# Turning the attention output, the spatial weights and part of q by DMA transposes instead of TensorE transposes, with more products on GpSimd and a split tail

## The chip, the cores and the metric

One core of one Trainium2 chip. The metric is device time in microseconds (us) of one execution. A kernel is always compared with the kernel before it, run in the same rounds on the same chip. Single executions fall into a fast and a slow state (the kernel before: about 170.5 us, or about 173 us with a lower granted TensorE clock); only the times of fast ones are compared. The granted clock is the share of full speed at which the chip lets TensorE run, 1.00 being full speed.

## The reference, cut to what matters

```python
# attention: 4 batches, 8 heads, 768 rows, head width 64, blocks of 96 rows
P = sort_net                                   # 8x8 per head, five row/column normalisations
for _ in range(5): P = exp(P - max); P /= rows; P /= columns
k_sorted = einsum('bhij,bhjcd->bhicd', P, k_blocks)     # v likewise
attn = softmax(scale * q_b @ k_sorted^T)                # inside a block of 96
x = (attn @ v_sorted)                                   # -> (4, 768, 512)
# gated MLP
h = relu(x @ w_in);  u, v = halves of h                 # 512 each
v_n = (v - mean) / sqrt(var + 1e-6)
v_s = einsum('ts,bsd->btd', w_spatial, v_n) + b_spatial # 768x768 spatial weights
out = (u * v_s) @ w_out
```

TensorE contracts over partitions. So `x` has to be turned before it meets `w_in`, `w_spatial` before it meets `v_n`, and q and k before the scores. Who does the turning is what the change is about.

## The kernel before: the parts that the change and the argument touch

The schedule is a string of units, given to the engines in this order. A unit is `name : PSUM bank : engine that evicts (A ScalarE, D VectorE, P GpSimd) : arguments`. `L` loads, `QT` turns a pair of q heads, `KT` and `VM` mix k and v with the sort matrix, `VC` rearranges v by small DMAs, `SC` and `AT` are scores and attention output, `XT` turns x, `WS` the spatial weights, `VP` and `UP` are the two halves of the first projection, `LA` normalises v, `SP` is the spatial product with bias and gate, `OP` the output. Other names in the cuts do not matter to the argument.

```python
# order, cut: batch 0's end and batch 1's start
AT:1:0:2:1 XT:7:A:0:0:1 PD:1:4:8 PD:1:0:4 AT:5:0:3:1 ... WS:3:D:3 WS:4:A:0
WS:1:D:1 WS:7:A:2 AT:5:0:1:1 L:k:1:0:128 XT:0:A:0:1:1 WS:3:D:4 VP:2:D:0:2 WS:4:A:5 ...
# order, the tail
SP:1:D:3:1 SP:4:D:3:3 SP:1:D:3:0 SP:4:D:3:2 OP:4:A:3:0 OP:1:D:3:1 OP:4:A:3:2

def u_WS(ps, eng, n):                     # 6 TensorE transposes, one eviction
    for c in range(G):
        nc.tensor.transpose(t[:, 0, c*128:(c+1)*128], wsp_nat[:, c, n*128:(n+1)*128], ident)
    copy(eng, wspT[:, n], t[:, 0, 0:S])

def u_QT(ps, eng, b, hp, ih):             # 12 matmuls against the identity, one eviction
    ...
def u_XT(ps, eng, b, ih, kp):             # 8 TensorE transposes of 96x128, one eviction
    ...
def u_L(what, *a):                        # loads: all issued by GpSimd, in its order
    nc.gpsimd.dma_start(...)
def u_VC(b, ih):                          # v rearranged: 4 small DMAs, issued by SyncE
    for i in range(ih*NI, ih*NI+NI):
        nc.sync.dma_start(out=..., in_=vm[b % 2][i*TB:(i+1)*TB]...)
def u_AT(ps, b, hp, ih):                  # product with 1/sum always on VectorE
    ...
def u_LA(b, n):                           # normalisation always on VectorE
    ...
```

The softmax here doesn't subtract the row's maximum and nothing guards it: scores larger than these inputs give would overflow.

## Time and profile before

| | before |
|---|---|
| time, median of 4 runs | 170.54 us (170.31 to 170.74) |
| span in the profile, mean TensorE clock | 170.2 us, 0.972 |
| TensorE busy | 149.7 us, 88% |
| GpSimd busy | 34.0 us, 20% |

The profile is of one execution, which took 171.97 us; its span, from the first to the last instruction, is 170.2 us. The page's main rows are shown in the prediction below. Two more lines of the page of before matter later: the packet sizes, and the queue that SyncE's DMAs go through (packets, MB, share of 16 engines' span).

```profile
DMA packets 21027, 21.59 MB, mean 127 GB/s; under 512 B 912, under 2 KB 17808, under 8 KB 21008
q1 hardware_dynamic: 6144, 9.13, 16.8%
```

And three windows of 5 us of before (start and end, length; busy us and number of instructions of TensorE, weight loads, VectorE, ScalarE, GpSimd; granted clock; DMA share; GB/s moved). TensorE is busy throughout at full clock, while the loads run at 205 GB/s or more.

```profile
35.00:40.00 5.00, 4.95 (x56) 3.26 (x55) 3.78 (x8) 3.92 (x6) 0.00 (x0) 1.00 1.30 205
40.00:45.00 5.00, 4.95 (x46) 2.75 (x46) 4.34 (x9) 4.02 (x7) 0.88 (x1) 1.00 1.29 205
45.00:50.00 5.00, 5.00 (x90) 3.43 (x89) 4.02 (x8) 4.66 (x9) 0.00 (x0) 1.00 1.24 255
```

### The profile page before, as it was taken

Reading aid. Unit: us, or ns where it says so; the run is one execution under the profiler, and the core shown is the slowest. Engines: PE = TensorE matmul, PEld = TensorE weight load, DVE = VectorE, ACT = ScalarE, POOL = GpSimd, SP = SyncE. Lnnn points to the kernel's source line nnn. Section 1 sums busy time; section 2 is a strip of 40 time slices with the busy share of each in tenths; the row PEclk is TensorE's granted clock in tenths of the full one; section 3 lists DMA queues with packets and bytes.
Section 4 is the critical chain, followed back from the end, with each engine's and each line's share of the span. In section 5 each row is a group of like instructions: output and inputs, shape, how many; then the busy total and the mean of one; then the engine's idle time right before and its main releaser. Section 6 shows DMA issues by size and latency. Waiting matters only on the chain.

```text
span 170.2 us, 4241 instructions
## 1 busy us (share of the span) xinstructions
PE 149.7 (88%) x1785; PEld 95.4 (56%) x1797; DVE 122.8 (72%) x253; ACT 89.6 (53%) x133; POOL 34.0 (20%) x41
## 2 busy tenths in 40 slices
PE   0485697999999999999999999999999999999660
PEld 0344586984756668745557566655557644455320
DVE  3784775787879789778896898569788649739420
ACT  3414676676998519656569134476653247520120
POOL 7929913202000035050000030300003300000000
PEclk9999997599999999999999999999999999999996
DMA  2999999999999992929333000823240000360063
GB/s 28 164 191 204 207 214 203 205 203 207 212 275 231 214 234 23 178 24 161 123 129 123 4 0 9 149 36 123 96 155 0 4 0 0 123 247 4 0 231 143
DMA packets 21027, 21.59 MB, mean 127 GB/s; under 512 B 912, under 2 KB 17808, under 8 KB 21008
## 3 DMA queue, kind: packets, MB, share of 16 engines
q0 software_dynamic: 14864, 12.19, 46.5%
q1 hardware_dynamic: 6144, 9.13, 16.8%
q8 instruction: 14, 0.23, 0.5%
q14 instruction: 5, 0.04, 0.1%
HBM read 24.78 MB, written 6.29 MB: 183 GB/s over the span
## 4 chain that ended last, share of the span: by engine, by line
PE 76%; DMA 8%; DVE 7%; issue 3%; ACT 2%; POOL 2%; ACTq 0%; POOLq 0%; DVEq 0%
PE ps L483 15%; PE ps L471 12%; PE ps L430 12%; PE ps L504 10%; DMA v_in<-in_v_dram 7%; PE ps L389 5%; PE ps L366 5%; PE ps L293 4%; PE ps L411 4%; PE ps L278 3%; DVE gt L495 2%; DVE z L489 2%; DMA out_dram<-o_sb 2%; PE ps L338 2%; PE ps L326 2%
## 5 line engine op out<-in xcount | busy, mean ns | idle before, releaser
L374 ACT ACTIVATE ex<-ps 96x768 bf16<-96x768 f32 x32 | 24.6, 804 | 17.7 <-PE ps L366 17.0
L483 PE MATMUL ps<-wspT,v_sb 128*128 128x384 bf16 x192 | 33.4, 326 | 0.0
L495 POOL TENSOR_TENSOR gt<-z,u_sb 128x768 bf16<-128x768 f32 x7 | 11.5, 1643 | 80.7 <-DVE rec L396 44.5
L483 PEld LDWEIGHTS <-v_sb 128*128 128x128 bf16 x192 | 18.1, 98 | 11.5
L504 PE MATMUL ps<-w_out_sb,gt 128*128 128x512 bf16 x91 | 21.8, 379 | 2.0 <-DVE z L489 1.1
L471 PE MATMUL ps<-xT,w_in_sb 128*128 128x384 bf16 x128 | 23.0, 326 | 0.0
L397 DVE TENSOR_TENSOR x_sb<-ps,rec 96x512 bf16<-96x512 f32 x32 | 22.0, 686 | 1.1
L430 PE MATMUL ps<-w_in_sb,xT 128*128 128x512 bf16 x89 | 21.8, 379 | 0.5 <-issue 0.2
L108 ACT COPY o_sb<-ps 128x1024 f32<-128x1024 f32 x11 | 11.1, 1011 | 19.5 <-PE ps L504 16.6
L489 DVE TENSOR_TENSOR z<-ps,b_bc 128x768 f32<-128x768 f32 x16 | 15.3, 956 | 7.4 <-PE ps L483 7.4
L444 DVE BATCH_NORM_STATS2 stats<-v_sb 128x6 f32<-128x512 bf16 x24 | 16.3, 679 | 3.2 <-ACT v_sb L114 2.9
L471 PEld LDWEIGHTS <-w_in_sb 128*128 128x128 bf16 x128 | 11.9, 98 | 7.9
L278 PE MATMUL ps<-ident,q_in 128*64 128x128 bf16 (+1 forms) x240 | 8.4, 217 | 8.3 <-DMA q_in<-in_q_dram 6.4
L504 PEld LDWEIGHTS <-gt 128*128 128x128 bf16 x96 | 8.8, 97 | 11.7 <-DVE gt L495 1.4
L114 ACT ACTIVATE u_sb<-ps 128x768 bf16<-128x768 f32 x12 | 9.7, 811 | 10.1 <-PE ps L471 9.9
L430 PEld LDWEIGHTS <-xT 128*128 128x128 bf16 x96 | 8.9, 98 | 9.3
L389 PE MATMUL ps<-vb,ex 96*128 96x65 bf16 x256 | 12.8, 199 | 0.1
L389 PEld LDWEIGHTS <-ex 96*128 96x128 bf16 x256 | 11.1, 101 | 2.6 <-issue 0.3
L278 PEld LDWEIGHTS <-q_in 128*64 128x64 bf16 (+1 forms) x240 | 6.9, 115 | 9.8 <-DMA q_in<-in_q_dram 6.4
L116 DVE TENSOR_SCALAR v_sb<-ps 128x1024 bf16<-128x1024 f32 (+1 forms) x7 | 8.0, 1147 | 5.5 <-PE ps L430 5.3
L366 PEld LDWEIGHTS <-kT 64*96 64x96 bf16 x256 | 8.0, 124 | 5.3 <-issue 3.9
L366 PE MATMUL ps<-qT,kT 64*96 64x96 bf16 x256 | 10.7, 215 | 0.2 <-ACT ex L374 0.2
(73 smaller groups left out, 197.5 us busy)
## 6 DMA issues: line engine op xcount, KB each, us to landing
out_dram<-o_sb SPq DMA_DIRECT2D x12, 512.0 KB, 2.8
k_in<-in_k_dram POOLq DMA_DIRECT2D x4, 768.0 KB, 14.3
v_in<-in_v_dram POOLq DMA_DIRECT2D x4, 768.0 KB, 21.9
vb<-vm SPq DMA_DIRECT2D x24, 99.0 KB, 5.5
q_in<-in_q_dram POOLq DMA_DIRECT2D x3, 768.0 KB, 20.4
wsp_nat<-in_moe_w_spatial_dram POOLq DMA_DIRECT2D x1, 1152.0 KB, 21.6
w_in_sb<-in_moe_w_in_dram POOLq DMA_DIRECT2D x2, 512.0 KB, 14.7
q_in<-in_q_dram POOLq DMA_DIRECT2D x2, 384.0 KB, 8.7
```

Source lines behind the costliest of these rows:

```text
L278: nc.tensor.matmul(t[hh * 64:hh * 64 + 64, g * n:(g + 1) * n], lhsT=st["q", b][lo:lo + n, 2 * hp + hh, g * D:(g + 1) * D], rhs=ident[lo:lo ...
L366: nc.tensor.matmul(t[0:BLK, hh, ii * BLK:(ii + 1) * BLK], lhsT=kT[rows, i * BLK:(i + 1) * BLK], rhs=qT[rows, i * BLK:(i + 1) * BLK], start ...
L374: nc.scalar.activation(out=e[:, 0:2 * NI * BLK].rearrange("p (h c) -> p h c", h=2), in_=t[0:BLK, :, 0:NI * BLK], func=AF.Exp, scale=scale,)
L389: nc.tensor.matmul(t[:, hh, ii * VW:ii * VW + D + 1], lhsT=e[:, c:c + 128], rhs=vb[b % 2][:, ih * NI + ii, 2 * hp + hh, 0:D + 1], start=Tr ...
L397: nc.vector.tensor_mul(out=x_sb[:, :, hp * 128:hp * 128 + 128].rearrange("p i (h d) -> p h i d", h=2), in0=tv[:, :, :, 0:D], in1=_raw_ap(r ...
L430: nc.tensor.matmul(t[:, x, :], lhsT=st["xT", b][:, kc, n * 128:(n + 1) * 128], rhs=w_in_sb[:, kc, DH:DFF], start=(kc == 0), stop=(kc == KC ...
L444: nc.vector.bn_stats(out=stats, in_=v_sb[:, x, :])
L471: nc.tensor.matmul(t[:, x, 0:HW], lhsT=w_in_sb[:, kc, mc * 128:(mc + 1) * 128], rhs=st["xT", b][:, kc, ih * HW:(ih + 1) * HW], start=(kc = ...
L483: nc.tensor.matmul(t[:, x, 0:HW], lhsT=st["v_sb", b, n][:, mc * 128:(mc + 1) * 128], rhs=wspT[:, n, x * HW:(x + 1) * HW], start=(n == 0), ...
L489: nc.vector.tensor_add(out=z.rearrange("p (x c) -> p x c", x=2), in0=t[:, :, 0:HW], in1=b_bc.rearrange("p (x c) -> p x c", x=2),)
L495: eng.tensor_mul(out=gt, in0=z, in1=st["u", b, mc // 2][:, mc % 2])
L504: nc.tensor.matmul(t[:, x, :], lhsT=st["gt", b, mc][:, c * 128:(c + 1) * 128], rhs=w_out_sb[:, mc, :], start=(mc == 0), stop=(mc == FC - 1),)
```

## The change

The intent: TensorE bounds the middle of the kernel, and part of its work is turning data. DMA engines, mostly idle after 62 us, can turn data while they move it. So all spatial weights, x of batches 1 to 3 and q of batches 2 and 3 are turned by DMA, issued by SyncE; ten attention products and most normalisations go to GpSimd, which was 20% busy; batch 0's q is loaded by halves of the heads; and the last spatial unit and the last outputs are halved to one PSUM bank each (`SH` and `OH` in the cut). The whole order was laid out anew. The core of the diff:

```diff
+    def u_WX(c):                       # six of these in place of six WS
+        nc.sync.dma_start_transpose(out=wspT[:, :, c*128:(c+1)*128], in_=wsp_nat[:, c, :])
+    def u_XX(b, ih):                   # six in place of twelve XT (batches 1 to 3)
+        nc.sync.dma_start_transpose(out=x_tile(b, ih)..., in_=st["x", b, ih]...)
+    def u_QX(eng, b):                  # two in place of eight QT (batches 2 and 3)
+        for hh in range(2): ...        # two copies put q in the order the DMA wants
+        nc.sync.dma_start_transpose(out=st["qX", b]..., in_=qx...)
 def u_AT(ps, eng, b, hp, ih):
+        if eng == "P":                 # ten of 32
+            nc.scalar.copy(out=xr, in_=tv[:, :, :, 0:D + 1])
+        (nc.gpsimd if eng == "P" else nc.vector).tensor_mul(...)
 def u_LA(eng, b, n):
+        if eng == "P":                 # fifteen of 24
+            nc.gpsimd.tensor_scalar(out=nm, in0=mv[:, n, 0:1], scalar1=-1.0, ...)
+            nc.gpsimd.tensor_scalar(out=v_sb, in0=v_sb, scalar1=nm, scalar2=rs, ...)
 # order, cut
-WS:1:D:1 WS:7:A:2 AT:5:0:1:1 L:k:1:0:128 ...
+PD:1:4:8 SC:6:0:2:1 ... PD:2:4:8 AT:2:D:0:1:1
+L:v:1:0:128 AT:6:P:0:2:1 SC:0:0:0:1 VT:4:D:3:0 L:k:1:0:128 ...
+SC:2:0:3:0 SC:0:0:1:0 PD:3:4:8 WX:5 ... AT:0:P:0:1:0 ... L:q:1:0:128 ... WX:3 ... WX:0
 # tail
-SP:1:D:3:1 SP:4:D:3:3 SP:1:D:3:0 SP:4:D:3:2 OP:4:A:3:0 OP:1:D:3:1 OP:4:A:3:2
+SP:0:D:3:1 SP:2:D:3:2 SP:0:P:3:0
+SH:2:D:3:3:0 SH:3:D:3:3:1 OH:0:A:3:1 OH:3:D:3:0 OH:2:A:3:4 OH:0:A:3:2 OH:3:A:3:3 OH:2:A:3:5
```

## The prediction

> **What bounds the kernel now.** I read the page first (busy time, then the 40 slices, then the chain that ended last), then the groups kept apart by shape, then the chain in order of time, and last the tail.
>
> ```profile
> PE 149.7 (88%) x1785; PEld 95.4 (56%) x1797; DVE 122.8 (72%) x253; ACT 89.6 (53%) x133; POOL 34.0 (20%) x41
> PE   0485697999999999999999999999999999999660
> PEclk9999997599999999999999999999999999999996
> DMA  2999999999999992929333000823240000360063
> ...
> PE 76%; DMA 8%; DVE 7%; issue 3%; ACT 2%; POOL 2%; ACTq 0%; POOLq 0%; DVEq 0%
> ```
>
> TensorE is at 9 tenths in nearly every slice from about 30 us to 157 us, and 76% of the chain is TensorE. So in the middle a TensorE instruction that goes is time that goes, if nothing makes TensorE wait in its place. The DMA engines are full to about 62 us (the loads of three batches and all weights) and mostly idle later. The head to 15.6 us is loads: the chain stands 11.5 us on v. The granted clock dips at 25 to 34 us.
>
> Busy time misleads for small matmuls: a transpose of x shows 215 ns, but they overlap. What a unit costs is read from the chain in order of time (columns: start us, us, what):
>
> ```profile
> 31.51 0.64 PE ps L411 x8
> 33.23 1.91 PE ps L257 x24
> ...
> 71.26 0.79 PE ps L411 x16
> ...
> 92.03 0.34 PE ps L278 x12
> ...
> 135.86 0.68 PE ps L411 x16
> ```
>
> A unit of 8 transposes of x costs 0.34 to 0.40 us at full clock (0.64 in the slow stretch), a q unit of 12 costs 0.34, and the 36 of the spatial weights cost 1.91 + 0.34 + 0.34 = 2.59 us.
>
> The tail is bound by VectorE, not TensorE:
>
> ```profile
> 151.56 0.97 DVE z L489
> 152.55 0.94 DVE gt L495
> ...
> 157.35 0.96 DVE z L489
> 158.33 0.97 DVE gt L495
> 159.30 0.05 issue
> 159.35 1.48 PE ps L504 x6
> 160.86 0.04 issue
> 160.90 1.02 ACT o_sb L108
> 161.94 2.76 DMA out_dram<-o_sb
> 164.79 1.01 ACT o_sb L108
> ```
>
> Four pairs of bias-add and gate go through VectorE one after the other while TensorE waits; then three two-bank outputs, two of them evicted by ACT in 1.01 us each. The last eviction also waits for an output buffer still being written out.
>
> **What the Trainium skill says.** (1) "Advanced Engine Details and Errata", X-Bar Transpose (TRN2): transposing DMAs run as fast as plain ones, 350 to 400 GB/s; "DMA: Bandwidth & Descriptors", Latency and other measured facts, has 261 GB/s for a non-contiguous case, and its Anatomy section a fixed cost near 2 us per DMA. Nothing in the trace before transposes by DMA; its plain 512 KB stores landed in 2.8 us and its small v rearrangements in 5.5 us (median), which fits a fixed cost plus queueing. (2) "GPSIMD Engine Reference", 4.1: two-input elementwise work is about twice as slow there, and GpSimd has no way into PSUM, which is why the moved attention products need a ScalarE copy first. The trace agrees: the gate took 1643 ns on GpSimd and 958 ns on VectorE. (3) "SBUF — State Buffer", on the shared port pair: a VectorE op in a two-port mode or with two SBUF inputs and a GpSimd op lock each other out. The GpSimd row before, 20% busy, does not show how much that costs.
>
> **The change part by part.**
>
> TensorE. x: 128 transposes become 32 (batch 0 keeps its four units). The chain pieces of the twelve units of batches 1 to 3 are 0.68 + 0.79 + 0.34 + 0.34 + 0.79 + 0.34 + 0.34 + 0.68 = 4.3 us. Spatial weights: 36 go, 2.6 us. q of batches 2 and 3: eight units of 0.34, 2.7 us. q of batch 0: eight half units become four full ones, of which the two that v's arrival does not hide save some 0.4 us. Added on TensorE: nothing; the scores of batches 2 and 3 read q in runs of 16 columns and all scores write to 128-column places, which I take as free. Sum: **10.0 us off the TensorE path**.
>
> VectorE. Off: 10 attention products of 0.686 (6.9), 15 normalisations of 0.404 (6.1), 4 x copies of 0.55 (2.2), 3 weight copies (1.7), 4 full and 4 half q copies (3.8 + 2.2), one v_sb relu (1.2): 24.1. On: three more full gates and two halves (3.9), 3 v copies, one each of u, vm, two outputs and the mix copy (5.4), and four copies of 128x1536 that put q in the order the DMA wants (estimate 1 us each, three times the 404 ns of a 128x512 one-input op and rounded down: 4). Net about -11, so 112 us of 159: 70%, as before, not a bound.
>
> ScalarE. Off: 8 x copies (6.4), 3 weight copies (2.4), 4 half q (1.9), others 7.7; on: ten copies of 96x520 from PSUM (0.58 each, from the 577 ns of its 96x512 copy: 5.9), five single-bank outputs (3.0), one relu (1.0). Net -8.5, to 81 us.
>
> GpSimd. Off: 4 gates of 1.64 (6.6). On: 10 products at 1.1 (two thirds of 1643 ns), 15 normalisations at 0.7 (its one-input 512-column copy took 622 ns) plus small negations: some 24. Net +17, to 51 us. Beside TensorE, unless a product it does is the last piece of an x block.
>
> DMA. Added: 6 weight transposes of 197 KB, 6 of x of 393 KB, 2 of q of 786 KB, 5.1 MB on SyncE's queue. Estimated landing, with 2 us plus bytes at 261 GB/s: 2.8, 3.5 and 5.0 us. The order leaves room: between the last attention product of an x block and its first reader stand some 7.6 us of TensorE work (for the last block three spatial units of 1.95 and a v pair of 1.73), less about 1 us for the product itself and its queue. q has over 10 us. The weight transposes fall in the saturated stretch but the first spatial unit now comes later, after all of batch 1's attention.
>
> Tail. From the end of the first of the last spatial units, before: 170.2 - 151.5 = 18.7 us. After, with the same durations: three full units and two halves end TensorE's part at 5.9; GpSimd's gate of unit 0 starts at 4.9 and ends at 6.5, VectorE's last half gate at about 6.9 but only the second half of the rows needs it; six single-bank outputs of 0.865 from 6.6 end at 11.8; a one-bank copy 0.6; a 256 KB store some 2.4; and the 1.6 us that also follow the last landing before: 16.4. **2.3 us** off.
>
> Sum: 170.4 - 10.0 - 2.3 = 158.1. I put back about 1 us: waits that the removed work had covered (in the batch-0 stretch at 19 to 30 us TensorE is already only 70 to 80% busy, so some of what goes there goes into idle time). **159 us**.
>
> **Rivals.** (a) A transpose takes the place of the transposes: the wait for a landing replaces the 0.34 us units. For: eight transposes lie on the path by data, SyncE issues in order, so one x block stands behind four v rearrangements that wait for their own inputs, and the small v copies took 5.5 us rather than 2. Against: 7.6 us of cover. If a landing takes 10 us, four late ones cost 2.5 us each: 169. (b) The saturated DMA stretch binds: 1.2 MB of weight transposes push back the loads of batch 1. By bytes at the observed rate those loads come some 5 us ahead of their use now; the transposes would take 3 to 6 us of that, and TensorE gets there sooner. If half of it shows: 162 to 163. Against: several of those readers stand later in the new order. (c) GpSimd becomes the bound in places: a product there takes a copy (0.58), a reciprocal (0.2) and 1.1 us instead of 0.9, behind normalisations and 0.9 us DMA issues, and under the port lock. For: the normalisations feed the spatial units directly. Against: 32% busy. It would cost 1 to 3 us: 160 to 162. (d) Better than the sum: the VectorE stop at 50.9 to 53.6 us (u, then k, then vm on the chain, 2.7 us) and two stops inside units that show no releaser (1.9 and 1.0 us) go as well: 155.
>
> **Range and chances.** The sum of what goes rests on chain pieces, so it is good to 1 us; (b) and (c) each have perhaps one chance in four, (a) in its full form one in twelve, (d) in part one in three. That gives 159, and 155.3 to 163 for eight in ten. Faster by over 2% (below 167) needs only a third of the sum: 0.95; within 2%: 0.04; slower: 0.01.
>
> **What would show it.** Right: TensorE's busy time falls to about 140, its slices stay at 9 from about 35 us to the tail, the chain has no line for transposed x, q or weights above 1 us, landings of x stay below 6 us, the tail from the first of the last spatial units to the end is near 16.4 us. Wrong: TensorE idle before the v or u projections with a DMA into xT as releaser (a), or before batch-1 mixes with k or v loads (b), or before spatial units with GpSimd's v_sb or the products' x_sb (c); score matmuls of batches 2 and 3 slower than 0.25 us a unit.

## The result, and the profile after

| | before | after |
|---|---|---|
| time, median of 4 runs | 170.54 us | 179.78 us (178.58 to 181.51) |
| span of the profiled execution, mean TensorE clock | 170.2 us, 0.972 | 179.7 us, 0.922 (slow state) |
| ratio of fast runs, 95% interval | | 1.0519 (1.0455 to 1.0583) |

A ratio here is the mean time of one kernel's fast runs over the mean of the other's fast runs of the same rounds, so it is not quite the ratio of the medians. The result is correct in both. The change made the kernel 5% slower; the prediction was 159 us and gave "slower" one chance in a hundred.

The profiled execution of after is its slowest, in the slow state: 181.51 us, where the three fast ones took 178.58 to 180.24. The big waits read from it below are not of that state: e4, further down, has the same order up to 65 us, was profiled in the fast state and waits 9.96 us on q, 1.84 on v and 2.47 on k. From the page of after:

```profile
PE 145.6 (81%) x1506; PEld 88.0 (49%) x1519; DVE 114.1 (63%) x230; ACT 81.9 (46%) x124; POOL 52.9 (29%) x77
PE   0395999981089459954999999999999999999890
PEclk9997999999669655897899999999999999999999
DMA  2999999999999999999995419795316610035044
...
DMA packets 41490, 26.67 MB, mean 148 GB/s; under 512 B 21377, under 2 KB 38273, under 8 KB 41473
...
q1 hardware_dynamic: 26608, 14.24, 39.2%
...
PE 46%; DMA 32%; issue 11%; POOL 4%; DVE 2%; POOLq 1%; ACT 1%; SPq 0%; ACTq 0%; DVEq 0%
```

Three things stand out (a slice is 4.5 us here). TensorE has holes between 40 and 85 us (slices 1 and 0, then 4 and 5, then 5 and 4), where the row before had 9 throughout; its clock falls after each hole. The DMA row stays at 9 to about 94 us instead of 64. And SyncE's queue now takes 39.2% of the DMA engines' time instead of 16.8%, for only 5.1 MB more, in 20,464 more packets; packets under 512 B grew by as many. DMA's share of the chain went from 8% to 32%.

Where TensorE stood still, from its timeline in after (start us, length us, line, operation, output<-inputs, count, and in brackets the idle time before it and what ended it). L320 is q, L384 and L335 mix v and k, L485 and L530 are the two projections, L542 is the spatial product:

```profile
39.82 1.48 PE L530 MATMUL ps<-xT,w_in_sb 128*128 128x384 bf16 x8
49.92 2.13 PE L320 MATMUL ps<-ident,q_in 128*64 128x128 bf16 x36 [8.62 <-DMA q_in<-in_q_dram]
...
60.90 0.82 PE L384 MATMUL ps<-v_in,pd 128*128 128x384 bf16 x2 [2.30 <-DMA v_in<-in_v_dram]
...
67.05 0.85 PE L335 MATMUL ps<-pd,k_in 128*64 128x128 bf16 x12 [1.98 <-DMA k_in<-in_k_dram]
...
70.73 3.38 PE L542 MATMUL ps<-wspT,v_sb 128*128 128x384 bf16 x12
...
83.25 0.39 PE L485 MATMUL ps<-w_in_sb,xT 128*128 128x512 bf16 x1 [4.42 <-DMA xT<-x_sb]
```

With one more of 0.77 us on k at 39.03 these are 18.1 us of waits on DMA. The timeline of before has none over half a microsecond after 30 us on a DMA; its own q unit follows without a wait:

```profile
45.35 1.62 PE L278 MATMUL ps<-ident,q_in 128*64 128x128 bf16 x48
```

The same windows as above, in after. TensorE is nearly empty from 41 to 50 us, and all that while the DMA engines are busy but move half as much as before:

```profile
35.00:40.00 5.00, 4.17 (x43) 2.29 (x43) 3.27 (x5) 2.79 (x6) 3.83 (x6) 1.00 1.38 116
40.00:45.00 5.00, 1.30 (x8) 0.59 (x6) 1.19 (x4) 1.91 (x3) 2.92 (x4) 1.00 1.57 101
45.00:50.00 5.00, 0.08 (x2) 0.08 (x4) 0.00 (x0) 0.00 (x0) 0.00 (x0) 0.60 1.36 144
```

What the transposes took is in the DMA issues of after (number, median us from issue to landing) and in SyncE's timeline, whose length here is the time that SyncE itself is held by issuing:

```profile
wspT<-wsp_nat SPq DMA_TRANSPOSE x6, 12.2
xT<-x_sb SPq DMA_TRANSPOSE x6, 4.0
qX<-qx SPq DMA_TRANSPOSE x2, 11.5
```

```profile
29.00 10.86 SPq L301 DMA_TRANSPOSE wspT<-wsp_nat  x4
...
69.45 1.28 SPq L188 DMA_TRANSPOSE xT<-x_sb  x1
72.40 15.40 SPq L181 DMA_TRANSPOSE qX<-qx  x1
...
106.42 3.55 SPq L181 DMA_TRANSPOSE qX<-qx  x1
```

A weight transpose landed after 9.6 to 15.9 us, where 2.8 had been estimated. Of the six of x, all but the first took 3.8 to 4.7 (3.5 estimated); the first, still among the loads, took 13.8. Of the two of q, one took 17.5 among the loads, and the other 5.5 at 106 us, when the loads were over (5.0 estimated). The estimates were those of idle DMA engines.

Last, GpSimd's timeline shows when loads were issued. In before, batch 1's q:

```profile
20.39 0.94 POOL L155 DMA_DIRECT2D q_in<-in_q_dram  x1
```

In after, the same load, with a moved product in front of it:

```profile
32.30 1.04 POOL L454 TENSOR_TENSOR x_sb<-xr,rec 96x512 bf16<-96x512 f32 x1 [2.51 <-DVE rec L453]
33.29 0.94 POOL L154 DMA_DIRECT2D q_in<-in_q_dram  x1
```

GpSimd runs in order: where a product waits for its reciprocal (2.51 us here, 5.06 at 24.70 us), the load behind it waits too. q of batch 1 is issued 12.9 us later than before, and its reader comes about 4 us earlier (the q unit could have started at 41.3 us instead of 45.35).

**The theories after the result.** (T1) The transposes of the weights, put among the loads, slow the loads and hold SyncE, which also issues the v rearrangements; (T2) the products on GpSimd delay the load issues; (T3) a transpose is late for its own reader (x at 83.25 us). The rival to T1: any 1.2 MB added among the loads would cost the same, or late weights as such do the damage.

### The profile page after: what moved, and what is told of

It is laid out like the page before. It is cut to its first block, busy times and chain, and to the rows that moved or that the text cites. A ratio compares the mean times of both kernels' runs of the same rounds, so it can differ in the third digit from the quotient of the medians.

```text
span 179.7 us, 3709 instructions
## 1 busy us (share of the span) xinstructions
PE 145.6 (81%) x1506; PEld 88.0 (49%) x1519; DVE 114.1 (63%) x230; ACT 81.9 (46%) x124; POOL 52.9 (29%) x77
## 3 DMA queue, kind: packets, MB, share of 16 engines
q1 hardware_dynamic: 26608, 14.24, 39.2%
## 4 chain that ended last, share of the span: by engine, by line
PE 46%; DMA 32%; issue 11%; POOL 4%; DVE 2%; POOLq 1%; ACT 1%; SPq 0%; ACTq 0%; DVEq 0%
DMA k_in<-in_k_dram 17%; PE ps L485 9%; PE ps L542 9%; DMA xT<-x_sb 8%; PE ps L530 7%; DMA v_in<-in_v_dram 6%; PE ps L591 6%; PE ps L335 4%; PE ps L442 4%; PE ps L417 3%; PE ps L372 2%; DMA out_dram<-oh_sb 1%; PE ps L577 1%; POOLq L634 1%; PE ps L384 1%
## 5 line engine op out<-in xcount | busy, mean ns | idle before, releaser
L542 PE MATMUL ps<-wspT,v_sb 128*128 128x384 bf16 x180 | 32.2, 335 | 0.0
L485 PE MATMUL ps<-w_in_sb,xT 128*128 128x512 bf16 x87 | 23.0, 400 | 5.3 <-DMA xT<-x_sb 4.4
L454 POOL TENSOR_TENSOR x_sb<-xr,rec 96x512 bf16<-96x512 f32 x10 | 10.5, 1045 | 49.4 <-DVE rec L453 48.5
L530 PE MATMUL ps<-xT,w_in_sb 128*128 128x384 bf16 x128 | 23.5, 326 | 0.0
L542 PEld LDWEIGHTS <-v_sb 128*128 128x128 bf16 x180 | 17.5, 100 | 11.9 <-issue 1.3
L516 POOL TENSOR_SCALAR v_sb<-v_sb,nm,rstd 128x512 bf16<-128x512 bf16 x15 | 11.9, 792 | 28.4 <-ACT rstd L507 18.6
L548 DVE TENSOR_TENSOR z<-ps,b_bc 128x768 f32<-128x768 f32 x15 | 14.3, 953 | 8.5 <-PE ps L542 8.3
L320 PE MATMUL ps<-ident,q_in 128*64 128x128 bf16 x96 | 5.0, 267 | 15.0 <-DMA q_in<-in_q_dram 15.0
L591 PE MATMUL ps<-w_out_sb,gt 128*128 128x512 bf16 x69 | 16.6, 379 | 0.2
L485 PEld LDWEIGHTS <-xT 128*128 128x128 bf16 x96 | 9.1, 102 | 15.3 <-DMA xT<-x_sb 4.8
L454 DVE TENSOR_TENSOR x_sb<-ps,rec 96x512 bf16<-96x512 f32 x22 | 15.1, 687 | 0.8
L530 PEld LDWEIGHTS <-w_in_sb 128*128 128x128 bf16 x128 | 11.8, 98 | 7.8
L107 ACT CAST vm<-ps 128x768 bf16<-128x768 f32 x9 | 7.0, 803 | 13.1 <-PE ps L384 13.1
L113 ACT ACTIVATE v_sb<-ps 128x1024 bf16<-128x1024 f32 (+1 forms) x7 | 6.7, 962 | 11.5 <-PE ps L485 11.4
L554 DVE TENSOR_TENSOR gt<-z,u_sb 128x768 bf16<-128x768 f32 x12 | 11.6, 968 | 0.4
L320 PEld LDWEIGHTS <-q_in 128*64 128x64 bf16 x96 | 4.0, 140 | 16.0 <-DMA q_in<-in_q_dram 15.3
L107 ACT CAST qT<-ps 128x768 bf16<-128x768 f32 x7 | 5.4, 799 | 13.6 <-PE ps L320 13.6
## 6 DMA issues: line engine op xcount, KB each, us to landing
w_in_sb<-in_moe_w_in_dram POOLq DMA_DIRECT2D x2, 512.0 KB, 15.9
```

The costliest lines, as they stand in the source:

```text
L107: nc.scalar.copy(out=out, in_=in_)
L454: (nc.gpsimd if eng == "P" else nc.vector).tensor_mul(out=x_sb[:, hp].rearrange("p i (h d) -> p h i d", h=2), in0=tv[:, :, :, 0:D], in1=_r ...
L485: nc.tensor.matmul(t[:, x, :], lhsT=x_tile(b, n // 3)[:, kc, n % 3 * 128:(n % 3 + 1) * 128], rhs=w_in_sb[:, kc, DH:DFF], start=(kc == 0), ...
L516: nc.gpsimd.tensor_scalar(out=v_sb, in0=v_sb, scalar1=nm[:, 0:1], scalar2=rs[:, n:n + 1], op0=ALU.add, op1=ALU.mult)
L530: nc.tensor.matmul(t[:, x, 0:HW], lhsT=w_in_sb[:, kc, mc * 128:(mc + 1) * 128], rhs=x_tile(b, ih)[:, kc], start=(kc == 0), stop=(kc == KC ...
L542: nc.tensor.matmul(t[:, x, 0:HW], lhsT=st["v_sb", b, n][:, mc * 128:(mc + 1) * 128], rhs=wspT[:, n, x * HW:(x + 1) * HW], start=(n == 0), ...
```

## The experiments

Fourteen kernels gave a result, all correct. Diffs named "order" change only the string of units. All times:

| run | what it is | median us | ratio to before, 95% interval |
|---|---|---|---|
| e1_ws_on_pe | after, weights on TensorE | 174.11 | 1.0205 (1.0161 to 1.0249) |
| e2_before_plus_wx | before, weights by DMA | 186.64 | 1.0931 (1.085 to 1.1012) |
| e3_no_gpsimd_products | after, products on VectorE | 180.40 | 1.0588 (1.0529 to 1.0646) |
| e4_x_q_on_pe | after, x and q on TensorE | 193.87 | 1.1372 (1.1328 to 1.1416) |
| e5_ws_x1_on_pe | e1, batch 1's x on TensorE | 174.00 | 1.0102 (1.0017 to 1.0186) |
| e7_dummy_turn_late | before, dummy transposes at 90 us | 171.35 | 1.0032 (1.0 to 1.0063) |
| e8_dummy_copy_in_loads | before, dummy copies among loads | 175.84 | 1.0268 (1.0198 to 1.0339) |
| e9_dummy_turn_in_loads | before, dummy transposes there | 186.99 | 1.0949 (1.0926 to 1.0972) |
| e10_dummy_turn_after_vb | as e9, behind batch 1's v | 176.63 | 1.0289 (1.0215 to 1.0362) |
| f0_tail_only | before, split tail | 171.42 | 0.9864 (0.978 to 0.9949) |
| f1_late_turns_tail | f0, late x and q by DMA | 169.29 | 0.988 (0.9763 to 0.9997) |
| e11_no_gpsimd_no_early_turns | e5, products on VectorE | 175.65 | 1.0304 (1.0231 to 1.0378) |
| e12_loads_ahead | e5, loads issued ahead | 169.82 | 0.9939 (0.9913 to 0.9966) |
| e13_placed | e12, turns placed anew | 165.26 | 0.9705 (0.9678 to 0.9732) |

Before ran at medians of 170.45 to 170.95 us beside them. The medians include slow runs (two of four in f0 and in f1); the ratios do not.

### Which transposes cost: the weights back on TensorE

```diff
 # order, from after
-WX:5 ... WX:3 ... WX:0 ... WX:2 ... WX:4 ... WX:1
+     ... WS:7:D:0 ... WS:0:A:1 ... WS:2:D:2 WS:3:A:3 ... WS:0:D:4 ... WS:4:A:5
```

> The changed kernel with the six DMA transposes of the spatial weights given back to TensorE (6 units of 6 transposes, 2.6 us), all else as changed. Theory L (transposes of the weights take DMA time from the loads while these fill the DMA engines, and q, v and k of batches 1 and 2 come late): the 8.6 us wait for q at 41 to 50 us goes, the landing of the loads is back near that of the kernel before, and the time falls from 179.8 to 160 to 167 us. Theory X (the x and q transposes and the in-order SyncE queue are what costs): stays above 174. Theory G (GpSimd's products stand in front of the load issues and delay them): stays above 174.

Measured: 174.11 us, by the ratios 5.4 us less than after (1.0519 less 1.0205, of 170.5), though TensorE got 36 transposes back. It missed 160 to 167 us. The wait of 8.62 us on q is gone; the one on x is not. TensorE's and SyncE's timelines of e1:

```profile
42.55 1.20 PE L320 MATMUL ps<-ident,q_in 128*64 128x128 bf16 x36
...
74.59 3.60 PE L485 MATMUL ps<-w_in_sb,xT 128*128 128x512 bf16 x8 [6.11 <-DMA xT<-x_sb]
```

```profile
61.42 3.60 SPq L188 DMA_TRANSPOSE xT<-x_sb  x1
65.13 9.98 SPq L181 DMA_TRANSPOSE qX<-qx  x1
```

The first x transpose was issued at 61.42 us, 7 us before TensorE had come to its reader (68.48), and landed 13.1 us later; the DMA engines moved 191 GB/s from 65 to 70 us. So T1 and T3 both hold, for the same reason: the time at which a transpose runs. The loads show T1 directly. They were issued at the same times in both kernels, to 0.2 us (batch 1's q at 33.48 us in e1 and 33.29 in after, batch 2's v at 35.16 and 34.97), and landed 8 to 11 us earlier in e1: batch 1's q at 41.9 us and not 49.9, v of batch 2 at 52.6 and not 60.9, its k at 56.4 and not 67.0.

### The weights by DMA alone, in the kernel before

```diff
 # order, from before
-WS:3:D:3 WS:4:A:0 WS:1:D:1 WS:7:A:2 ... WS:3:D:4 ... WS:4:A:5
+WX:0 WX:1 WX:2 WX:3 ... WX:4 ... WX:5
```

> The kernel before with one part of the change alone: spatial weights turned by six DMA transposes in the place of the TensorE units. Theory L: TensorE work falls by 2.6 us, but the loads of batches 1 and 2 land about 8 to 12 us later and TensorE waits for them: 174 to 182 us. Theory X or G: loads unharmed, 167 to 169 us.

Measured: 186.64 us, 9% slower than before, with nothing else changed, and worse than the 174 to 182 expected. SyncE's timeline of e2:

```profile
28.96 22.28 SPq L264 DMA_TRANSPOSE wspT<-wsp_nat  x6
51.36 2.97 SPq L358 DMA_DIRECT2D vb<-vm  x4
```

SyncE was held for 22.28 us by six issues. Batch 1's v rearrangements, which in before go out at 41.94 us, go out at 51.36, and TensorE waits 4.54 us on them at 61.94 and in several smaller pieces after, besides 2.28 us on q and 3.19 on v. One part of the change by itself costs more than the whole change.

### Products back on VectorE

```diff
 # order, from after: every AT:_:P and LA:P
-AT:6:P:0:2:1 ... LA:P:0:4 ...
+AT:6:D:0:2:1 ... LA:D:0:4 ...
```

> The changed kernel with all attention products and normalisations back on VectorE (gates stay). Theory G: the loads are issued earlier, TensorE's waits for q, v, k go, 165 us or less. Theory L: the DMA engines are full either way, so earlier issue brings the loads no nearer: 176 to 182 us.

Measured: 180.40 us, as slow as after. But the waits moved. q of batch 1 is issued at 22.73 us instead of 33.29, and TensorE waits 1.04 us on it, not 8.62. In its place, from TensorE's timeline of e3:

```profile
52.17 0.20 PE L442 MATMUL ps<-vb,ex 96*128 96x65 bf16 x1 [3.13 <-DMA vb<-vm]
...
68.10 4.00 PE L542 MATMUL ps<-wspT,v_sb 128*128 128x384 bf16 x12 [3.81 <-DMA wspT<-wsp_nat]
```

So T2 is true of the q wait, which took both causes together: e1 removes it by taking the transposes away, e3 by issuing the load earlier. As the cause of the whole time, T2 alone falls. The last line also shows turned weights that came too late for their own reader, by 3.81 us.

### x and q back on TensorE, weights still by DMA

```diff
 # order, from after
-XX:1:1 QX:D:2 XX:1:0 QX:D:3 XX:2:1 XX:2:0 XX:3:0 XX:3:1
+XT:2:A:1:1:0 XT:6:D:1:1:1 ...  (two XT for each XX, four QT for each QX, at the same places)
```

> The changed kernel with x and q of batches 1 to 3 turned on TensorE again (12 units of 8 and 8 of 12 transposes, 7.0 us more TensorE work), the weights still by DMA. Theory L: the waits for q at 41 us and for v and k at 58 to 67 us stay, the 4.4 us wait for turned x goes, time 178 to 186. Theory X: waits after 65 us go, 168 to 174 us.

Measured: 193.87 us, outside the 178 to 186 that I had expected and on the bad side. The waits on q (9.96), v (1.84) and k (2.47 us) stay, so they are not from the x and q transposes; the wait on x's DMA goes. But the units that I put in its place stand right behind the products that feed them (TensorE waited 2.40 and 0.71 us there in batch 1), and they are 7 us of work (4.3 + 2.7). TensorE's busy time rose from 145.6 to 154.9 us, 9.3 of the 12.8 us between the spans of the two profiles (192.5 and 179.7); the rest is TensorE standing still, and was not split further. The run clears the late transposes of the early waits and no more.

### Weights and batch 1's x on TensorE

```diff
 # order, from e1
-XX:1:1 ... XX:1:0
+XT:2:A:1:1:0 XT:6:D:1:1:1 ... XT:2:A:1:0:0 XT:6:D:1:0:1
```

> The changed kernel with the weights and batch 1's x (four units) given back to TensorE; q of batches 2 and 3 and x of batches 2 and 3 stay on DMA. Theory L, now wider (any transpose by DMA issued before the loads are done, near 75 us, lands late and pushes the loads): the 6.1 us wait for turned x at 68 us and the low clock after it go, 163 to 168 us. Rival (what is left is GpSimd and the tail): stays at 172 to 175.

Measured: a ratio of 1.0102, still not faster than before, and outside the 163 to 168 us expected. Its interval overlaps that of e1, so the step from e1 is not clear of noise. No transpose is now among the loads before 65 us, and yet the loads dip. Windows of e5 (profiled in the slow state; the fast profile of e1 has 161 and 188 GB/s there):

```profile
35.00:40.00 5.00, 4.77 (x41) 3.00 (x43) 2.37 (x5) 2.33 (x5) 2.46 (x4) 1.00 1.20 163
40.00:45.00 5.00, 4.39 (x82) 3.35 (x83) 3.93 (x7) 4.57 (x7) 4.22 (x7) 1.00 1.18 187
```

163 and 187 GB/s, not 205, with GpSimd busy at products. That is T2 seen alone; e12 below tests it.

### Is it the transposing, the bytes, or the place? Three dummies in the kernel before

These keep the weights on TensorE and add six DMAs of the same 197 KB from `wsp_nat` into a tile that nobody reads. No reader can wait for them: what they cost is contention.

```diff
+    scr = const.tile([128, G, S], BF16, name="scr")
+    def u_DX(c):   # transpose
+        nc.sync.dma_start_transpose(out=scr[:, :, c*128:(c+1)*128], in_=wsp_nat[:, c, :])
+    def u_DC(c):   # plain copy of the same bytes
+        nc.sync.dma_start(out=scr[:, c, :], in_=wsp_nat[:, c, :])
 # e7: six DX together ahead of KT:0:A:3:2:2, at 90 us, the loads over
 # e8: one DC ahead of each WS;   e9: one DX ahead of each WS
```

> The kernel before plus six DMA transposes of the weights into a tile that nobody reads, issued near 90 us, when the DMA engines are mostly idle. Theory L: each lands in under 4 us and the time stays within 1% of before. If transposes by DMA are costly wherever they stand: over 2% slower.

> The kernel before plus six plain copies of the same 197 KB pieces, in rows of 1536 bytes, into a tile that nobody reads, issued when the weights have landed, in the load stretch. If only bytes count: 1.2 MB at the 205 KB a us of that stretch push the loads by 5.8 us, of which the slack of some 5 us covers most: 170 to 173 us. If these cost as much as the transposes: over 178.

> The same with six DMA transposes in place of the copies, in the load stretch, TensorE still turning its own weights. If transposing among the loads is what costs: 180 to 190 us, as with the weights turned only by DMA (186.6). If in that run the late weights themselves were what TensorE waited for: below 174.

SyncE's timeline and the DMA issues of e7 (transposes, idle DMA engines):

```profile
89.60 9.12 SPq L266 DMA_TRANSPOSE scr<-wsp_nat  x6
...
scr<-wsp_nat SPq DMA_TRANSPOSE x6, 3.7
```

of e8 (plain copies among the loads):

```profile
28.66 4.37 SPq L270 DMA_DIRECT2D scr<-wsp_nat  x6
...
scr<-wsp_nat SPq DMA_DIRECT2D x6, 192.0 KB, 7.2
```

of e9 (transposes among the loads), with TensorE's longest wait:

```profile
28.86 22.43 SPq L266 DMA_TRANSPOSE scr<-wsp_nat  x6
...
scr<-wsp_nat SPq DMA_TRANSPOSE x6, 14.3
...
62.01 0.24 PE L400 MATMUL ps<-vb,ex 96*128 96x65 bf16 x1 [6.08 <-DMA vb<-vm]
```

| six times 197 KB | SyncE held | median landing | GB/s at 35 to 45 us | cost by the ratio |
|---|---|---|---|---|
| transposes, late (e7) | 9.12 us | 3.7 us | | 0.5 us, at the edge of nothing |
| copies among loads (e8) | 4.37 us | 7.2 us | 265, 213 | 4.6 us |
| transposes among loads (e9) | 22.43 us | 14.3 us | 191, 157 | 16.2 us |

(The cost is the ratio less one, times before's 170.7 us.) The copies add to the traffic, 265 GB/s against before's 205; the transposes take away from it. So the rival "any bytes would do it" accounts for 4.6 of 16.2 us. (At 175.84 us, e8 is outside the 170 to 173 expected of bytes alone.) And e9 is as slow as e2 although its weights come from TensorE: late weights as such are not what made e2 slow.

Where is the rest? Not, at first, in the loads: batch 1's q landed at 45.0 us in e8 and 45.3 in e9 (40.8 in before), batch 2's v at 54.7 and 54.3 (48.1); only later loads came 4 to 5 us later in e9. What e9 has and e8 has not are waits of TensorE on the v rearrangements, 8.4 us in all, held up on SyncE behind the transposes; the next run takes these away. The two runs also differ in packet size, rows of 1,536 bytes for the copies and packets of 256 for the transposes, so turning and small packets are not told apart.

### The SyncE queue, or the DMA engines?

```diff
 # order, from before
-VC:1:0
+VC:1:0 DX:0 DX:1 DX:2 DX:3 DX:4 DX:5
```

> The kernel before plus the six dummy transposes, still in the load stretch, but issued on SyncE behind all eight rearrangements of batch 1's v rather than ahead of them. Theory Q (SyncE, held for some 22 us by six issues among the loads, keeps back the v rearrangements): batch 1's attention no longer waits for them; the wait moves to batch 2's, later and smaller: 172 to 178 us. Theory D (what costs is DMA time taken from the loads): loads land as late as in the other dummy run, 184 to 188.

Measured: a ratio of 1.0289, or 4.9 us. The six transposes still stand among loads and still hold SyncE, but now behind all of batch 1's v rearrangements. SyncE's timeline of e10:

```profile
48.55 19.69 SPq L266 DMA_TRANSPOSE scr<-wsp_nat  x6
```

TensorE's one wait on a rearranged v is 2.10 us (at 81.67, batch 2's). So of e9's 16.2 us about 11.3 go when nothing urgent stands behind the transposes on SyncE; the 4.9 that stay are the size of what plain copies cost. The two places are 20 us apart, with other loads in flight, so the split is for this case and not to the microsecond. In after itself the weight transposes held SyncE from 29.00 to 39.86 us and the v rearrangements went out at 39.99 us, not later than in before (41.94). Two of the next four went out some 5 us later than in before (51.66 and 52.52), but TensorE waited on none; so there T1 worked by way of the loads. By bytes alone, all 1.2 MB at 205 GB/s would push a load by 5.8 us (an estimate), and e1's loads came 8 to 11 us earlier than after's. No run put plain copies into after's order, so how much of that is bytes is not shown.

### The tail by itself, and the transposes that come late

```diff
 # f0: before's order in after's code, with only the tail changed
-SP:1:D:3:1 SP:4:D:3:3 SP:1:D:3:0 SP:4:D:3:2 OP:4:A:3:0 OP:1:D:3:1 OP:4:A:3:2
+SP:1:D:3:1 SP:4:D:3:2 SP:1:P:3:0 SH:4:D:3:3:0 SH:6:D:3:3:1 OH:1:A:3:1 OH:3:D:3:0 ... OH:4:A:3:5
 # f1: f0, and after the loads only: XX for x of batches 2 and 3, QX for q of batch 3
-XT:0:A:2:1:0 ... (eight XT)  QT:2:D:3:2:2 ... (four QT)
+XX:2:1 XX:2:0 XX:3:1 XX:3:0  QX:D:3
```

> The changed code with the order of units of the kernel before, and of the change only the tail: last spatial unit in halves, six single-bank outputs, one gate on GpSimd. No transposes by DMA, no other products moved. All theories: the tail part of the prediction holds, some 1.9 to 2.3 us off: 168.1 to 168.8 us. If the split tail had cost: 170.5 or more.

> As the tail-only run, plus the transposes by DMA that fall after the loads: x of batches 2 and 3 (eight units off TensorE, 2.9 us) and q of batch 3 (four units, 1.4 us). Theory L (transposes hurt only among the loads): each lands in 4 to 6 us, no wait above 1 us, 163.5 to 166 us, faster than both kernels. If turning by DMA is a loss wherever it stands: 168 or more.

f0's two fast runs took 168.80 and 169.24 us, a ratio of 0.9864: 2.3 us (0.9 to 3.7 by the interval), the size predicted for the tail. f1's took 167.99 and 168.06, a smaller gain than the 163.5 to 166 expected. Its transposes landed near the first estimates (x 3.9 us, q 5.7; 3.5 and 5.0 estimated), and only one was waited for: 1.29 us on x of batch 3, at 131.66 us.

The intervals of f0 and f1 overlap, so a gain of the late transposes over f0 is not shown by these runs; with two fast runs each they are too few for one microsecond.

### Loads issued ahead of the products

```diff
 # order, e12 from e5
-L:k:1:0:128  L:q:1:0:128  L:wo  L:v:2:0:128  L:k:2:0:128  L:q:2:0:128   (where they stood)
+L:v:1:0:128 L:k:1:0:128 L:q:1:0:128 L:wo
+AT:2:P:0:2:0 L:v:2:0:128 L:k:2:0:128 L:q:2:0:128
 # e11 from e5: every AT:_:P to AT:_:D, every LA:P to LA:D
```

> The changed kernel with weights and batch 1's x on TensorE (as in the run at 174.0), and the six load issues of k and q of batch 1, the output weights and v, k, q of batch 2 moved ahead of GpSimd's products in GpSimd's own order; no other engine's order changes. Theory G2 (with the transposes out of the way, GpSimd's products in front of the load issues let the loads run dry at 33 to 45 us, 154 to 188 KB a us where 204 is the full rate): the dip goes, v and k of batch 2 land 2 to 4 us earlier, and 3 to 6 us are saved: 166 to 170. If issue order is nothing: 171 to 175.

> The same kernel without the moved load issues, but with all attention products and normalisations back on VectorE, which also frees the issues. Theory G2: no dip, 166 to 171. If the GpSimd products helped by sparing VectorE: slower than the run with only the issues moved by 2 us or more. If neither matters: 171 to 175.

e12 took a ratio of 0.9939 where e5 had 1.0102, which is 2.8 us (1.6% of 170.7; by the two intervals some 1.3 to 4.3 us). Its windows:

```profile
35.00:40.00 5.00, 4.81 (x42) 2.98 (x43) 2.38 (x5) 2.34 (x5) 0.53 (x1) 1.00 1.29 205
40.00:45.00 5.00, 4.45 (x83) 3.43 (x83) 4.06 (x7) 4.67 (x7) 3.32 (x6) 1.00 1.27 221
```

The loads run at full rate with the products still on GpSimd, only behind the issues. e11 also frees the issues, by moving the products to VectorE; its loads run at full rate too (206 and 211 GB/s), and it is slower (1.0304): the waits of TensorE that end with a product's x_sb add up to 7.8 us there and to 3.1 us in e12. So GpSimd was a fit place for the products, and the order of its queue was the fault. What e12 still loses is in the places that I chose for the turns: 2.40 us before an x unit, 1.37 behind a weight eviction, and more.

### Placed anew

```diff
 # order, from e12: weights into the stretch from 35 to 45 us, each behind other work;
 # batch 1's x a few units behind its last product
+UP:0:A:0:0:1 WS:7:D:0 ... WS:0:A:4 VP:6:D:0:0:1 WS:4:A:1 ... UP:0:A:0:1:0 WS:7:D:5 ... WS:2:D:2 WS:3:A:3
+SP:4:D:0:3 XT:2:A:1:1:0 XT:6:D:1:1:1 ... VM:2:A:3:2 XT:6:D:1:0:1 ... VP:0:D:1:4:5 XT:6:A:1:0:0
```

> As the run with the load issues moved ahead (169.8), with the TensorE units that I gave back set where their evictions are free: weights at 35 to 45 us, batch 1's x one or two spatial units after its last product. If the rest of the predicted gain was lost to my placement (some 7 us of waits of TensorE on DVE and ACT evictions at 33 to 69 us in that run's trace): 163 to 167, faster than the before-order kernel with late transposes (168). If it was not: 168.5 to 171.

Measured: 165.26 us (164.92 to 165.60) against 170.57, a ratio of 0.9705: faster than both kernels. By the ratios, the way from after to here is 5.4 us for the weights on TensorE (e1), 1.8 for batch 1's x (e5), 2.8 for the loads ahead (e12) and 4.0 for the new places. From the page of e13:

```profile
PE 143.0 (88%) x1574; PEld 88.6 (54%) x1587; DVE 116.4 (71%) x235; ACT 85.2 (52%) x129; POOL 52.8 (32%) x77
PE   0295999998898969996999999999999999999790
...
PEclk9999599999999999999999999999999999999999
```

TensorE's row has no slice under 6 between 20 us and the tail, and the clock stays up after 20 us. It keeps the split tail, the products on GpSimd, q of batches 2 and 3 and x of batches 2 and 3 by DMA. One transpose is still waited for (1.20 us on q of batch 2, which holds SyncE for 10.29 us from 59.06, among the last loads).

## Why the prediction was wrong

**TensorE's work: right.** About 10 us left TensorE. e13 bears it out to about 1 us: it has 36 weight and 32 x transposes more than after, 2.6 + 1.4 us by the chain pieces of the prediction (a third of its 4.3), and runs at a clock of 0.989; 143.0 less 4.0 is 139.0 us, where the prediction had 140. (The clocks of before, 0.972, and e13 differ, and the 1.91 us of the weights' pieces were read where TensorE ran at a low clock, so it is no closer than that.)

**Tail: right.** e1, which has after's tail, starts the first of the last spatial units' bias-adds at 155.82 us and ends at 172.6: 16.8 us against 16.4 predicted and 18.7 before; f0 shows 2.3 us by itself, with the interval given there.

**Prices of moved work: right.** A product on GpSimd took 1045 ns (1.1 us predicted), a normalisation 792 ns and its negation 214 (0.7 and a little), ScalarE's copy 588 ns (0.58), a q copy 602 ns (1 us, too high). A score matmul with q in runs of 16 columns took 205 ns, so that was free, as taken.

**The DMA step: failed.** "Estimated landing, with 2 us plus bytes at 261 GB/s: 2.8, 3.5 and 5.0 us" holds for idle DMA engines (e7 3.7; f1 3.9 and 5.7; after's later ones 3.8 to 4.7 and 5.5) and not among loads, where the runs show 9.6 to 17.5. I wrote myself that "the weight transposes fall in the saturated stretch" and yet gave them the figure of an idle stretch. The reason given, that their reader "now comes later", looked at the wrong reader: not the spatial unit but the loads and rearrangements that share engines and queue with them. And the fixed 2 us stands in the Anatomy section for DMAs that GpSimd issues; these were SyncE's.

**Rival (b): right mechanism, wrong size.** It said that the transposes push the loads back, sized by bytes at 3 to 6 us out of 5 us of slack. The waits before q, v and k mixes are the ones it named: 0.77 + 8.62 + 2.30 + 1.98 = 13.7 us. Two terms were not in it. Six transposes among the loads cost 3.5 times what plain copies of the same bytes cost in before's order (16.2 against 4.6 us), some 11.3 us of it gone once they stood behind the v rearrangements on SyncE (e10); and in after they pushed the loads by 8 to 11 us (e1). And the slack was gone already, since q's load was issued 12.9 us later (about 10.6 of it by the products: 33.29 us against 22.73 in e3): rival (c) looked for GpSimd's cost before products' readers and not before the loads in its queue. Its other ground, that "several of those readers stand later in the new order", was false for q, whose reader came 4 us earlier.

**Rival (a): came true once.** Its sign, TensorE idle before a projection with a DMA into xT, is there at 83.25 us, 4.42 us, for the one x block among the loads. The 7.6 us of cover was not enough for a landing of 13.8 us.

**The account of the profiled executions.** This is bookkeeping of two single executions, and after's is a slow one; the spans of its fast ones are 1 to 3 us shorter (176.8 to 178.5), and which piece shrinks there is not known. Before's span of 170.2 us less the predicted 10.0 and 2.3 leaves 157.9. Waits on DMA, none of them in that sum, add 18.1. TensorE's busy time is 145.6 us, not 139.7, 5.9 more: after the holes its clock goes to half speed, at 46.0 to 52.8, 59.7 to 73.4 and 83.6 to 87.0 us, where a spatial unit took 3.38 us at 70.73 instead of some 2.1. If all work at half speed took twice as long (the q unit's first 36 matmuls took 2.13 us in after and 1.20 in e1, 1.8 times), the loss would be 9.9 us in after and 3.4 in before, 6.5 more: an estimate, near the 5.9. Other stops of TensorE before the tail shrank from 3.4 to 1.0 us, rival (d)'s gain: less 2.4. That gives 157.9 + 18.1 + 5.9 - 2.4 = 179.5, against a span of 179.7. The Trainium skill ("TensorE: Matmul & The Clock Gate", Part 1: The HAM clock gate) says that the clock is gated by how busy TensorE has been; this trace agrees, with a clock of 0.60 in the window of the q wait and 0.50 from 60 to 70 us, a spatial matmul then taking up to 528 ns instead of 326. So a wait costs more than its length.

**What stays open.** Why a transpose does so badly beside loads was not found. The 20,000 added packets of 256 B took about 22 ns each with idle engines and 27 to 98 ns next to loads (means over stretches of 5 us in after's trace), and six issues held SyncE by up to 4.2 us each in after and 6.2 in e10; whether the small packets, the turning itself or the shared queues do it, no run tells apart.

## What to carry to other kernels

Before moving work to the DMA engines, read their row stretch by stretch and the queue that will issue it: six transposes that were nearly free in an idle stretch (0.5 us) cost 16 us in this kernel when put among loads and in front of other small transfers, and 4.9 us behind these. When an in-order queue that issues loads is given compute as well, put the issues first; that alone was worth some 1.3 to 4.3 us here. And count a wait on TensorE as more than its length, since the work after it runs at a lower clock.

## What the Trainium skill lacked or had wrong

- "Advanced Engine Details and Errata", X-Bar Transpose (TRN2): "TRN2 transpose DMAs are as fast as regular DMAs". Beside loads they were not: 14.3 us against 7.2 us to landing for the same 197 KB, and 16.2 against 4.6 us of the kernel's time (e9 and e8), most of the difference by way of the issuing queue (e10: 4.9 us). With idle engines 197 KB landed in 3.7 us, 393 KB in 3.9 and 786 KB in 5.7 (e7, f1); 393 KB more in 1.8 us is 218 GB/s (an estimate from these two).
- "DMA: Bandwidth & Descriptors", Issuing engines are not separate DMA queues: it calls the time to issue a DMA usually small beside the DMA. A transpose held SyncE for 1.3 to 3.9 us with idle engines and about 3.7 us (22.43 us for six), up to 15.40 us for a large one, among loads; behind it other DMAs waited. The page has no figure for a transpose issued while loads run.
- "GPSIMD Engine Reference", 4.1, puts two-input elementwise work at about twice VectorE's time. Here a product took 1045 ns on GpSimd and 687 on VectorE, 1.5 times (GpSimd's read a copy in SBUF, VectorE's read PSUM, so they are not quite the same work).
- No page that I read says that compute on GpSimd delays the loads that GpSimd issues: one load went out 10.6 us later here than with the products on VectorE (33.29 us in after, 22.73 in e3).
